# Mixing transform and capacity-limited expert layer on one core: tokens stored by transform call, expert phase in program order, and late tokens packed by top-8

## The chip, the cores and the metric

The kernel runs on one core of one Trainium2 chip. The metric is device time in microseconds (us), and lower is better. Medians are quoted with the range. Before the change the median was 743.34 us (742.24 to 746.65, three runs).

The engines are called as the profile calls them. PE is the matrix engine and PEld its weight loads, which overlap PE. DVE is the vector engine, ACT the scalar engine, POOL the general-purpose engine, and SP the engine that issues plain DMAs. Indirect DMAs, which gather or scatter rows by an index, are all issued from POOL here.

One warning for all numbers below: the runs fell on several chips, and the kernel before took about 742 us on some and about 702 us on others. Every verdict is therefore a ratio to the kernel before on the same chip in the same rounds, and absolute times are compared only within one chip.

## The reference, cut to what matters

```python
def _attn_ref(x):                         # x: 8 x 2496 x 256
    X = np.fft.fft(x, axis=1)
    X = np.fft.fft(X, axis=2)
    return X.real.astype(np.float32)

def _moe_ref(x, w_gate, w1, w2):          # 19968 tokens, 8 experts, 256 -> 1024 -> 256
    cap = N // E                          # 2496 tokens for each expert, exactly
    logits = x @ w_gate
    order = np.argsort(-logits.flatten())
    for idx in order:                     # best (token, expert) pair first
        tok, e = int(idx) // E, int(idx) % E
        if assigned[tok] >= 0 or counts[e] >= cap:
            continue
        assigned[tok] = e
        counts[e] += 1
    ...
    for e in range(E):
        mask = assigned == e
        out[mask] = np.maximum(x[mask] @ w1[e], 0.0) @ w2[e]
```

The input is the same draw each time (`np.random.seed(19597987)`).

## The kernel before

The kernel computes the transform as matmuls with cosine and sine tables and stores the tokens to DRAM (`t_dram`). It finds one threshold per expert in four rounds. A token sits in a grid of 128 partitions by 160 columns. After a part of the first round most tokens are already decided; they are the *early* tokens. Each early token's place is its rank among those of the same expert in the same pair of columns, and 24 places (`SW`) are kept per expert and pair. Whoever doesn't fit, or isn't decided yet, is *late*.

```python
# rank: for output partition k, count the chosen tokens in partitions p > k
nc.vector.tensor_scalar(rankb, in0=kgrid[:, 0:P], scalar1=iota_p, scalar2=None, op0=AL.is_lt)
...
# first_strips(): rank in one column, and for the second column of a pair all of the first on top
nc.tensor.matmul(rps, lhsT=rankb, rhs=ohb[...], start=True, stop=False)
nc.tensor.matmul(rps.rearrange("p (f s k) -> p f s k", s=2, k=NK)[:, :, 1, :], lhsT=onesb,
                 rhs=ohb[...][:, :, 0, :], start=False, stop=True)
...
nc.vector.scalar_tensor_tensor(has, in0=t3, scalar=float(SW), in1=sure, op0=AL.is_lt, op1=AL.mult)  # early
```

The transform's results go to `t_dram` through three stores per batch, and the negated copies have a tile of their own:

```python
st = stg.tile([P, NB, 2, D], BF, tag="stage", bufs=2, name="stage")
sn = stg.tile([P, NB, 2, P], BF, tag="stneg", bufs=2, name="stneg")
...
for b in range(NB):
    dst = td_q[kc, :, b0 + b].rearrange("p (g s) d -> p g s d", s=2)
    nc.sync.dma_start(dst[:, :, 0, :], st[:, b])
    nc.sync.dma_start(dst[:, :, 1, 0:P + 1], st[:, b, :, 0:P + 1])
    nc.sync.dma_start(dst[:, :, 1, P + 1:D], sn[:, b, :, 0:P - 1])
```

A *sort call* reloads 8 columns of tokens (`xl`) and moves them into expert order by matmuls with 0/1 marks (`pt`). The marks of one column are one contiguous row of 192 values:

```python
def sort_call(n):
    ...
    for g in range(4):
        pt = work_tile([P, 2, EW], BF, "pt", 4)
        for cc in range(2):
            nc.vector.tensor_scalar(pt[:, cc, :], in0=rampw, scalar1=spot[:, c:c + 1], scalar2=None,
                                    op0=AL.is_equal)
        for cc in range(2):
            for j2 in range(2):
                nc.tensor.matmul(sps[...], lhsT=xl[:, 2 * g + cc, j2 * P:(j2 + 1) * P],
                                 rhs=pt[:, cc, :], ...)
        take(dst[:, :, 4 * u + g, :], sps[...])
```

`take` evicts a matmul result on ACT or DVE, whichever a running count of work holds less busy. Then come 56 expert tiles of up to 384 tokens: 40 early ones out of the sorted strips, 16 late ones gathered from DRAM. A tile is 16 matmuls with `w1` (`hps`) and 24 with `w2` (`ops`); its result rows (`ot`) go out by three scatters. Between tiles, at fixed places (`aside`), the kernel runs the later rounds, the placing of the late tokens (`rest_step`) and the inverse of that placing (`place_step`), which tells each late slot its token:

```python
at(0, 3, finish_round)
for n in range(NROUND - 1):
    at(2 + 3 * n, 3, round_step)
at(11, 3, rest_step)
at(13, 3, place_step)      # inverse over all 160 columns, then the decode of the indices
G0 = 16                    # first gather of a late tile
```

A flag counts whatever went wrong, such as an expert over its capacity. If it isn't zero, a *fallback* behind `tc.If(unsettled > 0)` decides and computes again all tokens that are not early. It is always right, and slow.

## Time and profile before

| stage of the kernel before (profiled span 747.3 us) | us |
|---|---|
| tables, logits | 0 to 150 |
| transform, from where the weights load too | 150 to 259 |
| weight turns, first sorts | 259 to 286 |
| tiles 0 to 15, with the later rounds | 286 to 405 |
| no `hps` matmul at all (placing, inverse, decode) | 405 to 443 |
| the other 40 tiles | 443 to 747 |

The first lines to read are windows of the trace of the kernel before. The columns are: start and end, length, busy us of each engine with its number of instructions, granted clock of PE (1 is full), DMA share, GB/s.

```profile
core 0: us, PE busy (x) PEld busy (x) DVE busy (x) ACT busy (x) POOL busy (x), PEclk, DMA share, GB/s
202.00:259.00 57.00, 57.00 (x502) 49.33 (x500) 0.00 (x0) 22.37 (x53) 0.00 (x0) 0.97 0.52 121
...
286.00:400.00 114.00, 106.86 (x832) 74.23 (x832) 104.58 (x329) 84.02 (x249) 48.17 (x41) 0.94 0.32 90
400.00:441.00 41.00, 22.35 (x196) 18.95 (x194) 31.94 (x61) 4.56 (x19) 0.37 (x1) 0.60 0.01 4
...
500.00:615.00 115.00, 115.00 (x969) 88.10 (x967) 54.83 (x138) 67.79 (x157) 59.95 (x61) 1.00 0.26 86
615.00:690.00 75.00, 54.85 (x392) 39.45 (x391) 24.15 (x47) 23.71 (x57) 48.54 (x50) 0.89 0.19 59
```

From 286 to 400 DVE is busy 92% of the time: the rounds run there. In 400 to 441 POOL issues one DMA, because its next instruction is a gather that waits for the inverse. From 500 to 615 PE is the limit. From 615 to 690 PE idles a quarter of the time.

The POOL timeline of the kernel before (start, length, instruction, idle time before it and what ended that) shows the gather that waits, and the pace of indirect DMAs after it:

```profile
441.65 1.02 POOL L921 DMA_INDIRECT xg<-t_dram,ids_l  x1 [41.27 <-DVE wa L638]
442.97 0.98 POOL L921 DMA_INDIRECT xg<-t_dram,ids_l  x1 [0.30 <-issue]
444.26 0.95 POOL L921 DMA_INDIRECT xg<-t_dram,ids_l  x1 [0.30 <-issue]
```

Note how to read this: one indirect DMA counts 0.98 us busy, but the next starts 1.3 us after it.

In the chain of waits of the kernel before (start, length, what), the stores of the transform stand between 160 and 202:

```profile
168.07 8.91 DMA t_dram<-stage
...
177.00 9.35 DMA t_dram<-stneg
...
188.28 9.42 DMA t_dram<-stneg
```

The groups of instructions of the sort, kernel before (form, count, busy us, mean ns of one, idle time before and its causes):

```profile
L870 DVE TENSOR_SCALAR pt<-rampw,spot 128x192 bf16<-128x192 bf16 x160 | 39.5, 308 | 66.2 <-PE sps L875 60.7 <-DMA t_dram<-stneg 2.5 <-issue 1.1
L875 PE MATMUL sps<-pt,xl 128*128 128x192 bf16 x320 | 34.5, 255 | 7.6 <-DMA xl<-t_dram 3.5 <-ACT hb L783 2.3 <-DVE w1t L789 1.1
```

The mean of a pipelined matmul (255 ns) includes its latency. What a matmul costs in a stream is its start-to-start time. It follows from a burst on the PE timeline, here 16 sort matmuls without a gap:

```profile
508.98 1.48 PE L875 MATMUL sps<-pt,xl 128*128 128x192 bf16 x16
```

That is (1.48 - 0.255) / 15 = 0.082 us each. The Trainium skill, "TensorE: Matmul & The Clock Gate", section "Back-to-back issue gap", gives N / 2.4 + 2.5 ns for the gap of an isolated matmul at a warm clock, by which I estimate 82.5 ns for N = 192. The section says that in a stream of weight loads and matmuls the formula is off; this burst is such a stream, and yet its trace agrees with the formula.

### The profile page before, as it was taken

What the parts mean: (1) busy time and instruction counts of PE and PEld (TensorE: products, weight loads), DVE (VectorE), ACT (ScalarE), POOL (GpSimd) and SP (SyncE); (2) the same over time, 40 slices, a digit from 0 to 9 for tenths busy, and PEclk for the clock granted to TensorE, in tenths of its full rate; (3) what the DMA queues carried; (4) which work ended last, traced back from release to release, by engine and by line L of the source; (5) the groups of instructions that cost most, each with busy time, mean ns of one, the idle gap of its engine ahead of it and who ended that gap; (6) DMA issues with size and microseconds to landing.
All of it is one profiled execution on the core that took longest, in us unless ns stands there. A gap on an engine that the chain in (4) does not pass through costs nothing.

```text
span 747.3 us, 12493 instructions
## 1 busy us (share of the span) xinstructions
PE 585.3 (78%) x4496; PEld 414.1 (55%) x4496; DVE 396.5 (53%) x958; ACT 373.2 (50%) x878; POOL 330.7 (44%) x364
## 2 busy tenths in 40 slices
PE   0766766668699968998987475489999997767994
PEld 0322321657588835666664453267777775545773
DVE  3986884568000086988997860103564553323552
ACT  1677886442233444767875013277555442323552
POOL 8786722270000040534533027645545557665554
PEclk9999796889999997999999557789999999799998
DMA  8676510069954595422221002222311222111111
GB/s 273 229 217 188 188 31 0 2 111 190 176 118 116 123 225 141 118 76 71 92 74 59 1 21 89 82 83 94 120 69 64 76 73 71 55 54 62 62 56 50
DMA packets 82854, 74.71 MB, mean 100 GB/s; under 512 B 28195, under 2 KB 67149, under 8 KB 82784
## 3 DMA queue, kind: packets, MB, share of 16 engines
q0 software_dynamic: 23296, 42.10, 21.4%
q1 hardware_dynamic: 59488, 31.74, 16.2%
q8 instruction: 37, 0.61, 0.3%
q14 instruction: 33, 0.27, 0.1%
HBM read 51.26 MB, written 32.24 MB: 112 GB/s over the span
## 4 chain that ended last, share of the span: by engine, by line
PE 50%; ACT 13%; DVE 12%; issue 7%; DMA 7%; POOL 6%; another core or an unknown queue 3%; SPq 0%; POOLq 0%; DVEq 0%; ACTq 0%
PE hps L945 15%; PE ops L956 13%; PE fftps L807 8%; PE yps L270 5%; POOL out_dram L960 4%; DMA t_dram<-stneg 3%; PE sps L875 3%; ACT zball L255 2%; ACT cjunk L474 2%; DMA t_dram<-stage 2%; DVE o_lo L602 2%; ACT zt L269 1%; ACT hb L783 1%; PE inv_ps L618 1%
## 5 line engine op out<-in xcount | busy, mean ns | idle before, releaser
L956 PE MATMUL ops<-w2t,hb 128*128 128x256 bf16 (+1 forms) x1344 | 185.9, 281 | 2.8 <-ACT hb L783 1.9
L960 POOL DMA_INDIRECT out_dram<-ot,rid x120 | 127.6, 1064 | 126.2 <-ACT ot L783 72.0
L783 ACT ACTIVATE hb<-hps 128x384 bf16<-128x384 f32 (+1 forms) x303 | 138.1, 490 | 67.2 <-PE hps L945 48.6
L956 PEld LDWEIGHTS <-hb 128*128 128x128 bf16 (+1 forms) x1344 | 135.9, 102 | 41.7 <-issue 4.8
L945 PE MATMUL hps<-xs,w1t 128*128 128x384 bf16 x640 | 136.3, 341 | 19.7 <-ACT hb L783 7.1
L945 PEld LDWEIGHTS <-w1t 128*128 128x128 bf16 x896 | 89.3, 101 | 89.5 <-issue 52.3
L787 DVE TENSOR_SCALAR hb<-hps 128x384 bf16<-128x384 f32 (+1 forms) x145 | 79.0, 548 | 76.7 <-PE hps L945 47.7
L783 ACT ACTIVATE ot<-ops 128x256 f32<-128x256 f32 (+1 forms) x121 | 46.2, 382 | 134.9 <-PE ops L956 83.1
L870 DVE TENSOR_SCALAR pt<-rampw,spot 128x192 bf16<-128x192 bf16 x160 | 39.5, 308 | 66.2 <-PE sps L875 60.7
L270 PE MATMUL yps<-zt,g_sb 128*16 128x512 f32 (+1 forms) x96 | 48.6, 612 | 32.1 <-ACT zt L269 30.9
L921 POOL DMA_INDIRECT xg<-t_dram,ids_l x48 | 46.2, 962 | 56.8 <-DVE wa L638 41.3
L945 PE MATMUL hps<-xt,w1t 128*128 128x384 bf16 (+1 forms) x256 | 53.0, 335 | 20.1 <-issue 8.4
L960 POOL DMA_INDIRECT out_dram<-ot,rows_l x48 | 47.0, 979 | 39.9 <-ACT ot L783 29.4
L111 POOL DMA_INDIRECT xb<-in_x_dram,mir_i x40 | 51.5, 1288 | 20.3 <-issue 15.2
L810 ACT CAST stage<-fftps 128x512 bf16<-128x512 f32 x40 | 23.3, 584 | 68.7 <-PE fftps L807 35.5
L827 POOL DMA_DIRECT2D w1raw<-in_moe_w_dram x8 | 5.9, 734 | 114.7 <-PE wps L836 114.0
L807 PE MATMUL fftps<-zball,hi_cE 128*128 128x258 bf16 (+1 forms) x200 | 48.1, 279 | 8.5 <-ACT stneg L811 7.3
L807 PE MATMUL fftps<-zball,hi_sO 128*128 128x254 bf16 (+1 forms) x200 | 47.0, 275 | 0.0
L789 DVE CAST w1t<-wps 128x512 bf16<-128x512 f32 x11 | 7.5, 685 | 73.9 <-PE misc L515 73.7
L875 PE MATMUL sps<-pt,xl 128*128 128x192 bf16 x320 | 34.5, 255 | 7.6 <-DMA xl<-t_dram 3.5
L783 ACT ACTIVATE xs<-sps 128x384 bf16<-128x384 f32 x69 | 30.6, 492 | 16.5 <-PE sps L875 12.5
L267 PEld LDWEIGHTS tp<-identf,z 128*128 128x128 f32 x160 | 19.6, 157 | 33.7 <-issue 27.8
(296 smaller groups left out, 942.5 us busy)
## 6 DMA issues: line engine op xcount, KB each, us to landing
xl<-t_dram SPq DMA_DIRECT2D x20, 512.0 KB
xa<-in_x_dram SPq DMA_DIRECT2D x8, 1024.0 KB
t_dram<-stage SPq DMA_DIRECT2D x40, 128.0 KB
w1raw<-in_moe_w_dram POOLq DMA_DIRECT2D x8, 512.0 KB
w2t<-in_moe_w_dram POOLq DMA_DIRECT2D x8, 512.0 KB
t_dram<-stage SPq DMA_DIRECT2D x40, 64.5 KB
t_dram<-stneg SPq DMA_DIRECT2D x40, 63.5 KB
out_dram<-ot,rid POOLq DMA_INDIRECT x120
```

Source lines behind the costliest of these rows:

```text
L111: nc.gpsimd.indirect_dma_start(out=bv[0:n, i, :], out_offset=None, in_=x_pairs, in_offset=bass.IndirectOffsetOnAxis(ap=mir_i[0:n, b * NK + ...
L270: nc.tensor.matmul(yps[pb:pb + 2 * E, 0:nn, :], lhsT=g_sb[:, blk, :], rhs=zt[:, 0:nn, :], start=(blk == 0), stop=(blk == 1))
L783: nc.scalar.activation(dst, src, ACT.Relu if relu else ACT.Copy)
L787: nc.vector.tensor_scalar(dst, in0=src, scalar1=0.0, scalar2=None, op0=AL.max)
L807: nc.tensor.matmul(fps[:, :, d0:d1], lhsT=tabs_[r][:nv, i, ks], rhs=zball[:nv, b0:b0 + NB, 2 * i + r, d0:d1], start=(i == 0 and r == 0), s ...
L810: nc.scalar.copy(st[:, :, sg, :], fps)
L870: nc.vector.tensor_scalar(pt[:, cc, :], in0=rampw, scalar1=spot[:, c:c + 1], scalar2=None, op0=AL.is_equal)
L875: nc.tensor.matmul(sps[:, j2 * EW:(j2 + 1) * EW], lhsT=xl[:, 2 * g + cc, j2 * P:(j2 + 1) * P], rhs=pt[:, cc, :], start=(cc == 0 and j2 == ...
L921: nc.gpsimd.indirect_dma_start(out=xg[0:nr, q, :], out_offset=None, in_=t_dram, in_offset=bass.IndirectOffsetOnAxis(ap=d["ids"](q, nr), ax ...
L945: nc.tensor.matmul(hps[:, 0:n], lhsT=w1t[d["e"]][:, j2, fc * P:(fc + 1) * P], rhs=d["x"](j2), start=(j2 == 0), stop=(j2 == 1))
L956: nc.tensor.matmul(ops[0:nr, 0:D], lhsT=d["hid"][:, fc, b0:b0 + nr], rhs=w2t[d["e"]][:, fc, :], start=(fc == 0), stop=(fc == F // P - 1))
L960: put = nc.gpsimd.indirect_dma_start(out=out, out_offset=bass.IndirectOffsetOnAxis(ap=d["rows"](b0 // P)[0:nr], axis=0), in_=ot[0:nr, :], ...
```

## The change

The intent has four parts. (1) The transform writes each half call with one store in 1 KB runs from a ring of five buffers, so that stores hold up nothing. (2) One DVE instruction makes the marks of all 8 columns of a sort call. (3) The expert phase keeps program order on PE, DVE, ACT and POOL (`manual_schedule`; before, the language's own scheduler ordered each engine's instructions); the later rounds are generators cut at `yield`, and `pace()` runs a piece of about 1.4 us of DVE after each third of a tile. (4) The late tokens of each partition are packed by top-8 steps into 64 slots (`KC`), so that the inverse covers 64 columns rather than 160; if a partition has more, the flag is raised.

The diff, cut to its core (the conversion of the rounds to generators, index arithmetic and set-up moved to other places are left out):

```diff
+KC = 64
+SYNC = None
 ...
     def transform(n):
-        st = stg.tile([P, NB, 2, D], BF, tag="stage", bufs=2, name="stage")
-        sn = stg.tile([P, NB, 2, P], BF, tag="stneg", bufs=2, name="stneg")
         for sg in range(2):
+            st = stg.tile([P, NB, 2, D], BF, tag="stage", bufs=5, name="stage")
             ...
-        for b in range(NB):                       # three stores per batch
-            ...
+            nc.scalar.copy(st[:, :, 0, :], fps)
+            nc.scalar.activation(st[:, :, 1, P + 1:D], fps[:, :, P + 1:D], ACT.Copy, bias=0.0, scale=-1.0)
+            nc.gpsimd.tensor_copy(st[:, :, 1, 0:P + 1], st[:, :, 0, 0:P + 1])
+            nc.sync.dma_start(td_v[n].rearrange(...)[:, :, sg, :], st.rearrange("p b s d -> p b (s d)"))
 ...
+    def sort_mark(n):
+        marks[n] = work_tile([P, EW, 8], BF, "pt", 2)
+        nc.vector.tensor_tensor(marks[n], ramp8, spot[:, None, 8 * n:8 * n + 8].to_broadcast([P, EW, 8]),
+                                op=AL.is_equal)
-                                     rhs=pt[:, cc, :], start=(cc == 0 and j2 == 0), ...
+                                     rhs=pt[:, :, 2 * g + cc], start=(cc == 0 and j2 == 0), ...
 ...
     def settle_rest():        # was rest_step() and place_step()
+        nc.vector.tensor_scalar(sure, in0=sl["has"], ..., accum_out=full)     # late tokens of a partition
+        nc.vector.tensor_scalar(full, in0=full, scalar1=KC + 0.5, scalar2=None, op0=AL.is_gt)
+        nc.vector.tensor_tensor(over_n, over_n, full, op=AL.add)
+        set_flag(flag_i, over_n)
+        for r in range(KC // 8):
+            nc.vector.max(keys[:, 8 * r:8 * r + 8], key)
+            if r < KC // 8 - 1:
+                nc.vector.match_replace(out=key, in_to_replace=keys[:, 8 * r:8 * r + 8], in_values=key, ...)
+            yield 0.6
+        yield from inverse(hi_l, lo_l, pay_l, E * LB, KC)       # 8 columns per piece
 ...
-    G0 = 16
+    G0 = 28
+        at(j, 1, lambda d=d: (place_all(), gather(d)))          # runs whatever pieces remain
+    def pace():
+        credit[0] = min(credit[0] + 1.4, 1.4)
+        while credit[0] > 0.0:
+            c = next(todo, "end")
+            ...
+            if c is SYNC:
+                return
+            credit[0] -= c
+    with tc.manual_schedule(engines=MAN):
         ...
         experts(tiles + late, "rows_out", aside, 0, pace)
```

## The prediction

> **What bounds the kernel now** (page and stage windows of the profile; span 747.3 us).
>
> 1. 0–150 us: tables, logits. Almost unchanged.
> 2. 150–259: transform, 800 matmuls. From 202 they run back to back, 0.11 us each: 88 us would do. Between 160 and 202 the chain of waits shows stores of `stage`/`stneg` to DRAM (9 us each; two buffers) while weights load. About 18 us lost.
> 3. 259–286: weight turns; the first sort waits for stores and reloads (`xl`).
> 4. 286–745: 56 expert tiles. At full pace (500–615: PE busy 115 of 115, clock 1.00) a tile costs PE 16 x 0.163 + 24 x 0.107 = 5.2 us. Elsewhere that isn't kept:
>  - 286–400: threshold rounds; DVE busy 92%; about 7.9 us per tile.
>  - 400–441: rest and inverse, DVE and PE alternating; no expert matmul for some 33 us (clock 0.60).
>  - 441–500: four tiles in 59 us. POOL stood 41 us behind the first late gather (waiting for the decode), then issues gathers and scatters back to back, 1.3 us each.
>  - 615–690: POOL again, 6 x 1.3 = 7.8 us per tile; PE busy 55 of 75.
>
> **What the change does**
> - Stores: one per half call, 1 KB runs, five buffers; reloads in 4 KB runs. Price: a POOL copy of 258 elements per half, about 0.4 us (estimate from the 2048-element copy, 1.90), hidden. Transform should become PE-bound: -12 us; stage 3: -8.
> - Sort marks: 8 instructions of 0.31 us become one of about 0.95 (estimate from `o_lo`, 2048 elements in 1.22): -1.5 us of DVE per call.
> - The sort matmuls then read every eighth bf16, 16 B apart. The Trainium skill, "SBUF — State Buffer", note on cachelines, wants two hits per 16-byte line for full rate. The trace shows strided operands only in the inverse, at half clock, no penalty visible. If halved: +0.083 x 320 = 26 us; I count 6.
> - Inverse: 160 columns to 64 (8 pieces, 1.3 us DVE each), plus 8 top-8 steps of 0.6: about 10 us DVE less, and cut up.
> - Rounds paced, 1.4 us of DVE per third of a tile. By the yields I count 101 pieces; the first gather forces the remainder at tile 28 (after 84). A burst of about 15 us remains, where 33 were lost.
> - Late gathers start at tile 28, spaced, after the decode: the 441–500 loss (about 35) mostly goes. But POOL must do 48 gathers and 84 scatters from tile 28 on: 172 us at 1.3, against PE's 150. POOL bounds the end; 615–690 stays.
>
> **Sum.** Experts start at 265. Tiles 0–27: ACT+DVE work about 330 us over two engines, 6.9 us per tile: to 458. Burst 15. Tiles 28–55: 185. End 658.
>
> **Prediction: 658 us, 8 in 10 within 626 to 696; faster by over 2%: 0.94, within 2%: 0.03, slower: 0.03.**
>
> **What would show it.** No `t_dram` stores of 9 us in the chain at 160–202; last transform matmul near 245; first `hps` near 265; no 20 us without expert matmuls; tiles 0–27 at 6.5 to 7.2 us with DVE and ACT both above 80%; POOL above 85% from tile 28 to 48; sort matmuls' start-to-start at 0.083 us (no stride price) or more.
>
> **What would make it wrong.** In-order queues: a paced piece ahead of an eviction stalls PE each third of a tile (up to 696). The stride costing 26 us or more. POOL copies or the 1536-element ramp holding the transform or the first sort. More than 64 late tokens in a partition: the fallback runs, far slower. Or the rounds hide fully and tiles run near 6.0 (about 630).

## The result, and the profile after

The change doubled the time. All four runs of the kernel after, and the profiled run of the kernel before, are on record as fast.

| | median us | range | runs | profiled span, mean granted clock |
|---|---|---|---|---|
| before | 742.79 | 741.49 to 746.65 | 4 | 747.3 us, 0.901 |
| after | 1518.84 | 1515.55 to 1528.28 | 4 | 1518.6 us, 0.821 |

The ratio is 2.045, with a 95% interval of 2.033 to 2.057. A ratio here is the mean time of one kernel's fast runs over that of the other's fast runs of the same rounds, so it is not quite the ratio of the medians. The record of this set does not say whether its result is correct; e13_room72 below, which takes the same slow path, is correct.

The windows of the trace after, columns as before:

```profile
202.00:251.00 49.00, 49.00 (x443) 42.90 (x443) 0.00 (x0) 19.16 (x44) 9.00 (x22) 1.00 0.36 119
251.00:291.00 40.00, 32.55 (x99) 11.41 (x99) 12.48 (x20) 11.55 (x23) 7.03 (x8) 0.59 0.58 145
291.00:541.00 250.00, 243.59 (x1541) 145.81 (x1546) 152.34 (x369) 150.13 (x395) 90.53 (x84) 0.98 0.24 76
541.00:564.00 23.00, 6.87 (x62) 5.96 (x62) 18.51 (x63) 0.00 (x0) 0.88 (x1) 0.58 0.02 6
564.00:780.00 216.00, 179.19 (x1296) 126.17 (x1293) 88.68 (x200) 79.31 (x173) 130.87 (x132) 0.93 0.19 59
780.00:1000.00 220.00, 71.26 (x250) 37.57 (x251) 163.72 (x376) 26.75 (x134) 11.79 (x13) 0.50 0.02 4
1000.00:1518.00 518.00, 363.22 (x2475) 248.02 (x2472) 172.74 (x360) 143.36 (x299) 306.89 (x311) 0.82 0.24 30
```

Two things stand out. The work that should end the kernel is done by 780; 738 us follow, first 220 us of DVE work, then 518 us with POOL running 311 instructions, nearly all of them indirect DMAs. And from 251 to 541 PE is busy 276 of 290 us while a tile takes longer than before: PE is busy with something slow.

The groups of the trace after name both:

```profile
L1043 POOL DMA_INDIRECT out_dram<-ot,rows_c x160 | 159.4, 996 | 132.5 <-ACT ot L858 53.3 <-DVE ot L864 46.8 <-issue 24.1
L1004 POOL DMA_INDIRECT xg<-t_dram,ids_c x160 | 156.2, 977 | 276.7 <-DVE wa L671 204.8 <-issue 42.3 <-PE tp L1016 12.4
...
L952 PE MATMUL sps<-pt,xl 128*128 128x192 bf16 x320 | 114.1, 517 | 0.4 <-ACT ot L858 0.4
...
L938 DVE TENSOR_TENSOR pt<-ramp,spot 128x1536 bf16<-128x1536 bf16 x20 | 19.0, 950 | 0.6 <-POOL ramp L923 0.6
```

`ids_c` and `rows_c` exist only in the fallback: 160 gathers and 160 scatters there mean that the flag was raised. And the 320 sort matmuls, same count and shape as before, are busy 114.1 us in place of 34.5. The marks did become cheaper as intended: 0.95 us per call where 8 x 0.308 = 2.5 us stood.

The PE timeline after shows the sort matmuls at two clocks:

```profile
269.01 21.95 PE L952 MATMUL sps<-pt,xl 128*128 128x192 bf16 x64
...
403.62 2.88 PE L952 MATMUL sps<-pt,xl 128*128 128x192 bf16 x8
```

The burst of 8 gives (2.88 - 0.517) / 7 = 0.338 us start to start, 4.1 times the 0.082 of before; the granted clock there was 1.00 (402 to 408). The burst of 64 gives (21.95 - 0.517) / 63 = 0.340, and there the granted clock was 0.50 with PE shown busy 20.00 of 20 us (270 to 290). The same pace at half and at full clock suggests that the matmuls wait for their operand and not for the array; the experiments on the stride below test it.

### The profile page after: what moved, and what is told of

It is laid out like the page before. It is cut to its first block, busy times and chain, and to the rows that moved or that the text cites. A ratio compares the mean times of both kernels' runs of the same rounds, so it can differ in the third digit from the quotient of the medians.

```text
span 1518.6 us, 19800 instructions
## 1 busy us (share of the span) xinstructions
PE 1080.0 (71%) x7117; PEld 696.8 (46%) x7123; DVE 737.7 (49%) x1633; ACT 544.7 (36%) x1286; POOL 665.8 (44%) x729
## 5 line engine op out<-in xcount | busy, mean ns | idle before, releaser
L1039 PE MATMUL ops<-w2t,hb 128*128 128x256 bf16 (+2 forms) x2624 | 374.7, 289 | 84.2 <-issue 35.5
L862 DVE TENSOR_SCALAR hb<-hps 128x384 bf16<-128x384 f32 (+2 forms) x432 | 224.0, 535 | 332.8 <-PE hps L1028 171.0
L1039 PEld LDWEIGHTS <-hb 128*128 128x128 bf16 (+2 forms) x2624 | 272.4, 104 | 176.4 <-issue 108.5
L1028 PE MATMUL hps<-xt,w1t 128*128 128x384 bf16 (+2 forms) x1152 | 250.0, 349 | 81.9 <-DVE hb L862 40.1
L858 ACT ACTIVATE hb<-hps 128x384 bf16<-128x384 f32 (+2 forms) x464 | 210.3, 480 | 243.4 <-PE hps L1028 161.6
L1028 PEld LDWEIGHTS <-w1t 128*128 128x128 bf16 x1792 | 180.7, 104 | 215.9 <-issue 152.6
L1004 POOL DMA_INDIRECT xg<-t_dram,ids_c x160 | 156.2, 977 | 276.7 <-DVE wa L671 204.8
L1043 POOL DMA_INDIRECT out_dram<-ot,rows_c x160 | 159.4, 996 | 132.5 <-ACT ot L858 53.3
L858 ACT ACTIVATE ot<-ops 128x256 f32<-128x256 f32 (+2 forms) x184 | 70.7, 384 | 195.4 <-PE ops L1039 89.2
L952 PE MATMUL sps<-pt,xl 128*128 128x192 bf16 x320 | 114.1, 517 | 0.4 <-ACT ot L858 0.4
```

The costliest lines, as they stand in the source:

```text
L858: nc.scalar.activation(dst, src, ACT.Relu if relu else ACT.Copy)
L862: nc.vector.tensor_scalar(dst, in0=src, scalar1=0.0, scalar2=None, op0=AL.max)
L952: nc.tensor.matmul(sps[:, j2 * EW:(j2 + 1) * EW], lhsT=xl[:, 2 * g + cc, j2 * P:(j2 + 1) * P], rhs=pt[:, :, 2 * g + cc], start=(cc == 0 an ...
L1004: nc.gpsimd.indirect_dma_start(out=xg[0:nr, q, :], out_offset=None, in_=t_dram, in_offset=bass.IndirectOffsetOnAxis(ap=d["ids"](q, nr), ax ...
L1028: nc.tensor.matmul(hps[:, 0:n], lhsT=w1t[d["e"]][:, j2, fc * P:(fc + 1) * P], rhs=d["x"](j2), start=(j2 == 0), stop=(j2 == 1))
L1039: nc.tensor.matmul(ops[0:nr, 0:D], lhsT=d["hid"][:, fc, b0:b0 + nr], rhs=w2t[d["e"]][:, fc, :], start=(fc == 0), stop=(fc == F // P - 1))
```

## The experiments

Fifteen runs were made, in five groups; each group shares a chip and its runs of the kernel before. "Before here" is that kernel's median on the same chip. All timed runs were correct except one. The theories were these. Theory A: the doubling is the fallback, because the packing has too few slots per partition, and the rest is the stride of 16 bytes with which a sort matmul reads its marks. Rivals: the fallback runs for another reason (a bug in the packing, or an expert over capacity); the slow sorts come from program order, from waiting evictions or from the clock.

### Room for all late tokens: e1_room

```diff
-KC = 64
+KC = 88
-        ki = asg.tile([P, KC], I32, name="ki")
+        ki = wa[:, 3, 0:KC].bitcast(I32)          # scratch moved into rows of wa: SBUF was full
-        kt = [asg.tile([P, KC], I32, name="kt%d" % i) for i in range(3)]
-        some = asg.tile([P, KC], FT, name="some")
+        kt = [wa[:, i, 0:KC].bitcast(I32) for i in range(3)]
+        some = wa[:, 4, 0:KC]
```

> Room for 88 late tokens per partition in place of 64 (scratch tiles put into a free tile, so that it fits); else the changed kernel. Theory 'overflow': placing the reference's tokens by the kernel's rule gives 23 partitions with more than 64 late tokens, at most 79, so the flag is raised by the count alone. Then the fallback is gone, the result stays right and the time is about 788 us: the hot part's end at 778 plus three more inverse pieces of 1.74 us, three more top-8 steps of 0.77 us and the end of the program. Rival 'rounds': the paced rounds leave an expert over capacity, or an expert's list is too long; then the fallback stays and the time is 1525 us or more. In both cases the sort matmuls still start every 0.34 us.

Measured: 760.85 us (758.91 to 762.22), before here 701.64, ratio 1.0835 [1.080, 1.087]. No instruction of the fallback is in the trace. The expectation of 788 was stated for the slower kind of chip, so its absolute number does not apply here (on that kind, e14_room80 below took 801); what it said, no fallback and unchanged sort matmuls, held. Two things changed in this edit, the room and the scratch tiles; e13_room72 and e14_room80 tell them apart. With enough room the packing gives the right result, and the capacity of the experts was not the cause. The sort is unchanged at 114.1 us busy.

### The stride of the sort's marks: e2_s8, e3_s4, e4_s2

All three start from e1_room and change only how the marks lie in memory: a step of 8, 4 or 2 bytes between neighbours that one matmul reads, in place of 16.

```diff
-        marks[n] = work_tile([P, EW, 8], BF, "pt", 2)           # step 16 B
+        marks[n] = work_tile([P, 2, EW, 4], BF, "pt", 2)        # e2_s8: step 8 B
+        marks[n] = work_tile([P, 4, EW, 2], BF, "pt", 2)        # e3_s4: step 4 B
+        marks[n] = work_tile([P, 8, EW], BF, "pt", 2)           # e4_s2: contiguous
...
-                                     rhs=pt[:, :, 2 * g + cc], ...
+                                     rhs=pt[:, (2 * g + cc) // 2, :, (2 * g + cc) % 2], ...   # e3_s4
```

> As e1_room, with the marks of four tokens side by side instead of eight: the moving operand of the sort matmuls steps 8 bytes[...]. Theory 'stride'[...]: start-to-start falls from 0.34 us to between 0.083 and 0.17, the kernel to 705 to 735 us. Rival 'eviction' (the sort matmuls wait for PSUM buffers or for the in-order evictions): 0.34 stays and so does the time of e1_room, about 788.

> As e1_room, step 4 bytes[...]. Theory 'stride': start-to-start 0.083 us, kernel about 705 us (80 us less than e1_room). The VectorE mark has inner runs of two, so it may lose its fast rate: 0.95 us, at most 1.9. Rival 'eviction': about 788.

> As e1_room, marks contiguous for PE (step 2 bytes). Theory 'stride': start-to-start 0.083 us as in the kernel before; the VectorE mark gets an operand repeated along its inner dimension, so about 1.9 us (estimate from bt, 768 elements in 0.95) against 0.95, which is off the critical path in most tiles: about 707 us. Rival 'eviction': about 788.

Measured, all on the chip of e1_room; the start-to-start time is worked out from bursts of 8 (2.88, 1.54, 0.85 and 0.82 us long) in the way shown above. One burst of each of the last three, in the order 8, 4 and 2 bytes:

```profile
320.51 1.54 PE L955 MATMUL sps<-pt,xl 128*128 128x192 bf16 x8
...
300.34 0.85 PE L955 MATMUL sps<-pt,xl 128*128 128x192 bf16 x8
...
288.51 0.82 PE L952 MATMUL sps<-pt,xl 128*128 128x192 bf16 x8
```

| marks' step | sort, busy us | start to start, us | DVE per call, us | median us | ratio to before [95%] |
|---|---|---|---|---|---|
| 16 B (e1_room) | 114.1 | 0.338 | 0.95 | 760.85 | 1.0835 [1.080, 1.087] |
| 8 B (e2_s8) | 60.8 | 0.170 | 0.95 | 713.91 | 1.0175 [1.014, 1.021] |
| 4 B (e3_s4) | 34.7 | 0.085 | 0.95 | 693.21 | 0.9879 [0.984, 0.992] |
| 2 B (e4_s2) | 34.2 | 0.081 | 1.75 | 699.98 | 0.9970 [0.994, 1.000] |

The groups of e3_s4:

```profile
L955 PE MATMUL sps<-pt,xl 128*128 128x192 bf16 x320 | 34.7, 252 | 3.0 <-DVE pt L940 2.6 <-ACT ot L858 0.4
...
L940 DVE TENSOR_TENSOR pt<-rampm,spot 128x1536 bf16<-128x1536 bf16 x20 | 19.0, 949 | 0.0
```

The groups of e4_s2:

```profile
L938 DVE TENSOR_TENSOR pt<-rampw,spot 128x1536 bf16<-128x1536 bf16 x20 | 35.0, 1750 | 0.1
...
L952 PE MATMUL sps<-pt,xl 128*128 128x192 bf16 x320 | 34.2, 254 | 6.1 <-DVE pt L938 4.7 <-ACT cjunk L484 1.2 <-DVE s_cand L527 0.2
```

The price of a matmul follows the step, with program order and everything else unchanged: the stride is the cause, and the rivals for the sorts fall. The times of e3_s4 and e4_s2 came out 7 to 12 us below what was expected (about 705 and 707). From 16 to 4 bytes the busy time falls by 79 us and the whole kernel by 68 us. A step of 4 bytes is the best of the four, because the contiguous layout makes the DVE instruction slower (one operand is then broadcast along the inner axis; 1.75 against 0.95 us), and DVE is needed in this stage.

With both defects mended the kernel is only 1.2% faster than before, not the 11.5% that was predicted. The next question is where that gain went.

### The kernel before against itself, with a trace on the faster chip: b_again

No edit.

> The kernel before, unchanged, for its trace on this chip (its time was 743 us on the chip of the prediction and 702 on that of the first experiments). Ratio 1.00. Theory 'output buffers': the difference between chips lies in the last third, where evictions into the eight ot buffers wait for scatters to land; there the stage 500 to the end should show it, and the stages up to 500 us should agree within 10 us. Rival 'clock or DMA everywhere': all stages are shorter in proportion.

Measured: 702.44 us (700.65 to 705.07), before here 705.55, ratio 0.9974 [0.992, 1.003], span 700.1. So the difference between 742 and 702 us belongs to the chips. Its trace is the one to hold against those of the mended kernel. Counted from the first `hps` matmul, the tiles start at the same times as in the first trace, within 0.1 us, up to tile 15. Then this chip is 31 us ahead at tile 18, just after the first late gathers, 19 at tile 22, and 41 at the end. That is a partial miss: the expectation wanted agreement within 10 us up to 500 us and the whole difference after it. Windows of the trace of b_again:

```profile
400.00:425.00 25.00, 10.96 (x101) 9.85 (x100) 22.36 (x42) 0.00 (x0) 0.00 (x0) 0.59 0.00 1
425.00:500.00 75.00, 62.34 (x485) 47.46 (x485) 21.08 (x73) 41.44 (x105) 49.56 (x51) 0.86 0.32 95
625.00:697.00 72.00, 59.00 (x494) 46.20 (x491) 29.58 (x58) 29.17 (x69) 49.93 (x52) 0.98 0.23 73
```

### More of the rounds per third of a tile: e6_pace

From e3_s4, with the pieces larger, so that none is left when the first gather forces them.

```diff
-    G0 = 28
+    G0 = 26
-        credit[0] = min(credit[0] + 1.4, 1.4)
+        credit[0] = min(credit[0] + 2.4, 2.4)
```

> As e3_s4 (ratio 0.988), with 2.4 us of VectorE work let through per third of a tile in place of 1.4, and the first late gather at tile 26 instead of 28. By the yields the rest is then placed after 75 calls, at tile 25, so nothing is left to force. Theory 'burst' (the remainder forced at tile 28 stops the expert matmuls for the 33 us that e3_s4 shows at 475 to 515): about 20 to 30 us faster than e3_s4, ratio 0.95 to 0.96, no window of 10 us without expert matmuls. Rival 'evictions': longer pieces ahead of the evictions cost about as much per tile as the burst did, ratio 0.98 to 1.0.

Measured: 689.67 us (685.78 to 691.7), before here 705.55, ratio 0.9772 [0.972, 0.983]. The long stretch without expert matmuls is gone (between 400 and 560 no gap between `hps` matmuls exceeds 5.1 us), but tiles 0 to 25 now take about 8.3 us each, where they take 7.0 in e12_again below. Against the ratio of e3_s4 (0.9879, another chip) this is some 1.1%, about a third of the expected gain and nearer to the rival's range: the work of the rounds didn't vanish, it moved into the tiles.

### The scheduler's order in place of program order: e7_sched

From e3_s4.

```diff
-    with tc.manual_schedule(engines=MAN):
+    if True:
```

> As e3_s4, but the expert phase is ordered by the scheduler again instead of in program order (undoes that part alone). Theory 'order matters': the scheduler pulls the rounds, and with them the rest and the inverse, ahead and lets them hold PE, as in the kernel before: 10 to 40 us slower than e3_s4, ratio 1.00 to 1.05. Rival: the pieces carry all of the effect, the order none; within 1% of e3_s4.

Measured: 683.09 us (679.12 to 684.75), before here 705.55, ratio 0.9685 [0.963, 0.974]. That is a miss with the wrong sign: the part of the change that was meant to keep the engines in step costs about 2%. The theory that program order is what makes the pacing work falls.

### Without the packing: e8_nopack

From e3_s4; the inverse again covers all 160 columns, in paced pieces of 8.

```diff
-        for r in range(KC // 8):
-            nc.vector.max(keys[:, 8 * r:8 * r + 8], key)
-            ...
-        yield from inverse(hi_l, lo_l, pay_l, E * LB, KC)
+        hi_l = asg.tile([P, GC], BF, name="l_hi")
+        lo_l = asg.tile([P, GC], BF, name="l_lo")
+        nc.vector.scalar_tensor_tensor(hi_l, in0=sl["v"], scalar=1.0, in1=sl["has"], op0=AL.add, op1=AL.mult)
+        nc.vector.tensor_scalar(lo_l, in0=sl["lo"], scalar1=1.0, scalar2=None, op0=AL.add)
+        yield from inverse(hi_l, lo_l, payb, E * LB, GC)
```

> As e3_s4 without the packing by top-8: the inverse runs over all 160 columns in 20 pieces instead of 11 (undoes that part alone; no count can overflow). Nine more pieces of 1.74 us, less eleven top-8 steps of 0.77 and about 3 us of decoding the packed keys: 4 to 6 us slower, ratio about 0.995, if the packing is worth only what it saves; more than 15 us slower if the length of the forced burst costs doubly (PE clock falling to half while it lasts).

Measured: 699.69 us (697.94 to 702.96), before here 705.55, ratio 0.9936 [0.988, 0.999]. Against the ratio of e3_s4 on two other chips (0.9879, and 0.9895 below) the packing may be worth some 0.5%, about 4 us, as was expected, but the intervals overlap ([0.984, 0.992] and [0.988, 0.999]) and the chips differ, so this is not shown. It is also the part that brought the fallback.

### Placing spread over thirty tiles: e9_late30 and e10_late30s, with e12_again beside them

From e3_s4: the first gather at tile 30 and 1.8 us of DVE per piece, so that the pieces just run out in time. e10_late30s is the same in the scheduler's order. e12_again is e3_s4 without an edit, on this chip.

```diff
-    G0 = 28
+    G0 = 30
-        credit[0] = min(credit[0] + 1.4, 1.4)
+        credit[0] = min(credit[0] + 1.8, 1.8)
-    with tc.manual_schedule(engines=MAN):         # e10_late30s only
+    if True:
```

> As e3_s4 (room for 88, marks 4 bytes apart, program order), with 1.8 us of VectorE work per third of a tile in place of 1.4 and the first late gather at tile 30 instead of 28: by the yields the rest is placed after 88 calls, at tile 29.3, so nothing is left to be forced. Theory 'burst': e3_s4 lost 33 to 40 us at tile 28 to the forced remainder; most of it comes back, 655 to 670 us where e3_s4 takes 693. Rival 'evictions' (as e6_pace hinted): the larger pieces slow every tile before, 685 us or more.

> As e9_late30, ordered by the scheduler instead of in program order. e7_sched was 14 us faster than e3_s4 by the medians, so about 645 to 660 us if the two gains add; equal to e9_late30 if the scheduler's gain was only in the forced burst.

> The kernel of e3_s4 once more, so that the three others are compared with it on one chip: ratio 0.98 to 0.99 of the kernel before on a chip like the last two; about 0.96 on one like that of the prediction, where the kernel before loses some 40 us more in its late stage.

| before here 702.58 | median us | range | ratio to before [95%] |
|---|---|---|---|
| e12_again | 694.51 | 691.16 to 700.34 | 0.9895 [0.981, 0.998] |
| e9_late30 | 678.49 | 677.07 to 685.55 | 0.9645 [0.958, 0.971] |
| e10_late30s | 657.70 | 655.19 to 658.37 | 0.9361 [0.930, 0.942] |

e9_late30 was expected at 655 to 670 if the burst was the cost and at 685 or more if the larger pieces were; it fell between. e10_late30s was expected at 645 to 660 and hit. So larger pieces with a later first gather, which end the burst, were worth about 16 us on balance, and program order costs about 21 us here; e7_sched had shown the sign, with 14.

What the order costs can be read between 285 and 475. Windows and waits of e9_late30 (a wait line names the waiting instruction, the releaser, the total us, the times and the longest):

```profile
285.00:475.00 190.00, 174.63 (x1389) 127.31 (x1393) 149.68 (x392) 139.46 (x383) 78.27 (x75) 0.97 0.29 90
```

```profile
PE misc L491 <- ACT cnt_x L488: 5.3, 3, 2.5
```

The same of e10_late30s:

```profile
285.00:475.00 190.00, 186.97 (x1567) 141.78 (x1569) 149.19 (x398) 144.00 (x404) 89.09 (x83) 1.00 0.30 97
```

```profile
PE misc L491 <- ACT cnt_x L488: 0.9, 2, 0.6
```

In program order PE stands at a small matmul of a round (`misc`) until DVE and ACT have made its operand, with the expert matmuls queued behind it. In the scheduler's order other matmuls stand there. PE is busy 187 rather than 175 of 190 us, and the first 26 tiles take 176 us from the first `hps` matmul rather than 195. The two traces exaggerate a little: that of e9_late30 is the slowest of its five runs (685.55), that of e10_late30s the fastest of its four (655.19), and e10_late30s's transform, which the edit doesn't touch, ended 5 us earlier. The `misc` wait shown is one of several such waits; it alone does not make up the 12 us.

### Fewer gathers: e11_gather1

From e9_late30: each late tile gathers once and uses the rows three times. The result is wrong (relative error 0.44); only the time is of interest.

```diff
-        for q in range((d["n"] + P - 1) // P):
+        for q in range(1):
...
-                nc.tensor.transpose(tp[:, j2, q * P:q * P + nr], xg[0:nr, q, j2 * P:(j2 + 1) * P],
+                nc.tensor.transpose(tp[:, j2, q * P:q * P + nr], xg[0:nr, 0, j2 * P:(j2 + 1) * P],
```

> Wrong result on purpose: as e9_late30, but each late tile gathers only its first 128 rows and uses them three times, so POOL issues 16 gathers instead of 48 and all else stays. Theory 'POOL rate' (from the first late gather on, POOL's 1.28 us for each gather or scatter sets the pace): 32 x 1.28 = 41 us less POOL work, and the end comes 20 to 40 us earlier than in e9_late30, until PE's 5.2 us per tile takes over. Rival 'landing' (the eight output buffers wait for the scatters' own latency): the same time as e9_late30 within 8 us.

Measured: 666.95 us (666.47 to 675.67), before here 702.58, ratio 0.9530 [0.944, 0.962]. That is 12 us less than e9_late30 by the medians and 19 by the profiled spans (683.5 and 664.8; the first is of the slowest run of its set). By the medians it lies between the two theories, which expected 20 to 40 and at most 8. Late stage and waits of e9_late30:

```profile
575.00:650.00 75.00, 61.34 (x460) 45.31 (x459) 29.22 (x60) 26.10 (x60) 57.23 (x59) 0.91 0.24 71
```

```profile
ACT ot L858 <- DMA out_dram<-ot,rows_l: 32.6, 12, 4.9
```

Late stage of e11_gather1, and what is left of the same wait in that window:

```profile
575.00:650.00 75.00, 74.61 (x631) 59.04 (x628) 40.69 (x81) 38.74 (x81) 47.22 (x49) 1.00 0.20 66
```

```profile
ACT ot L858 <- DMA out_dram<-ot,rows_l: 0.7, 1, 0.7
```

This supports a mechanism of the late stage. In e9_late30 POOL runs 59 instructions in 75 us, nearly all of them indirect DMAs, one each 1.27 us, which is its full pace. Scatters queue behind gathers, so the `ot` buffers come free late; ACT waits up to 4.9 us for one, and the evictions behind it in ACT's queue wait too. Take 32 of the 48 gathers away, and PE goes from 61 to 75 busy of 75 us. The edit takes away POOL's issuing and the gathers' traffic at once, so which of the two delays the scatters is not shown.

### Where the threshold of the fallback lies: e13_room72 and e14_room80

e1_room with 72 and 80 slots, one look each (one execution, state unknown).

```diff
-KC = 88
+KC = 72          # e13_room72
+KC = 80          # e14_room80
```

> As e1_room with room for 72 in place of 88: the same edit of the scratch tiles, only the number differs. Theory 'overflow' (placing the reference's tokens by the kernel's rule gives at most 79 in one partition): 72 still overflows, the fallback runs, the result is right and the time is above 1400 us. Rival 'side effect' (the fallback went away in e1_room because of the moved scratch tiles, not of the room): about 760 us.

> As e1_room with room for 80. Theory 'overflow', with my maximum of 79: no fallback, right result, about 758 us. If the kernel's more cautious first choice leaves a partition with more than 80, the fallback runs and the time is above 1400 us; the count in my placement is then too low by one or two, and the theory holds with another maximum.

Measured: 1529.01 us with 72 slots, 801.05 with 80, the kernel before 742.21 on the same chip; both correct. The fallback's gathers and scatters are in the trace of the first and not in that of the second. The 758 us expected for 80 slots was the number of the faster chip. The rival "side effect" falls, for both kernels have the moved scratch tiles. The 728 us between them are the fallback's price. To say in advance where the threshold should lie, I placed the reference's tokens on the host by the kernel's rule. That gives 4761 late tokens, 37 per partition on average, but 23 partitions with more than 64 and a largest count of 79. (A second count on the host gave 4697, 37, 23 and 78; the kernel's own counts stand in no trace.) The threshold between 72 and 80 agrees with both.

### The best version on the slower kind of chip: e15_best

The kernel of e10_late30s, unchanged.

> The kernel of e10_late30s once more, on whatever chip comes. On a chip where the kernel before takes about 702 us: ratio 0.93 to 0.94, as then. On one where it takes about 742: its last stage is longer by some 30 us there too, as in e14_room80 (801 where e1_room took 761), so about 690 to 700 us, ratio 0.93 to 0.95.

Measured: 701.4 us (699.64 to 712.14; one of the four runs was slow), before here 742.81, ratio 0.9452 [0.936, 0.954] from the fast runs, as expected (0.93 to 0.95, about 690 to 700 us). So the change with the marks at a step of 4 bytes, 88 slots, the first gather at tile 30, 1.8 us per piece and the scheduler's order is 5 to 6% faster than the kernel before on both kinds of chip.

## Why the prediction was wrong

The prediction was 658 us with a range of 626 to 696; the result was 1518.84. The terms in order of size:

1. **The fallback, +728 us (shown: e1_room, e13_room72, e14_room80).** The step that failed is "More than 64 late tokens in a partition: the fallback runs, far slower." The prediction wrote this down as a risk and left it out of its 658. All slower outcomes together were given a chance of 0.03. The profile before doesn't show the count, but it needed no run. As an estimate from the layout: in a pair of columns about 32 of 256 tokens want each expert, for 24 places; the second column ranks behind the whole first one, and a low partition behind the higher ones. A token of partition 0 in a second column thus has around 31 ahead of it. There are 80 second columns, so the first partitions can have up to about 80 late tokens each, and the measured threshold between 72 and 80 fits. The average of 37 hides it. A limit that holds per partition has to be checked against the worst partition.

2. **The stride, +79 us of PE time, +68 us of the whole (shown: e1_room against e3_s4).** The prediction said: "If halved: +0.083 x 320 = 26 us; I count 6." The trace shows 0.338 us per matmul, not 0.166, so 0.256 x 320 = 82 us by start-to-start times, and most of it lay on the critical path, because PE was the limit in that stage. The mechanism was named and its term mis-sized. The prediction took from the Trainium skill, "SBUF — State Buffer", the note on cachelines, that the full rate needs two hits per 16-byte line. Here one hit per line costs 4.1 times, two hits still 2.1 times, and only four per line (4 bytes) come within 5% of the contiguous rate. Halving was the prediction's own assumption; the page only says that there is a penalty. And the inverse, in which the prediction saw none, could not have shown it: its matmuls have 48 columns and came one each 0.10 us (32 in 3.23 us in b_again), while the price found here, 0.338 / 192 = 1.76 ns per column, is 0.085 us for 48.

3. **What remains with both mended: 692.2 us (span of e12_again) where 658 was predicted.** The 658 was worked out from a trace of the slower kind of chip, and no run timed both mends there with this order and pace. An estimate from e14_room80's 801.05 less the 68 of the stride is 733 us, so about 75 us are missing there, not 34. The stages of e12_again are in these windows:

```profile
283.00:473.00 190.00, 178.85 (x1457) 132.35 (x1461) 144.24 (x346) 139.61 (x380) 86.69 (x81) 0.99 0.30 96
473.00:515.00 42.00, 20.07 (x153) 15.75 (x151) 33.89 (x122) 6.34 (x15) 7.02 (x7) 0.59 0.05 17
515.00:600.00 85.00, 85.00 (x713) 65.08 (x712) 47.20 (x96) 43.27 (x95) 63.64 (x65) 1.00 0.25 79
600.00:650.00 50.00, 39.12 (x294) 28.32 (x291) 17.97 (x38) 15.77 (x36) 38.08 (x39) 0.93 0.23 68
650.00:690.00 40.00, 31.35 (x263) 24.80 (x261) 16.32 (x33) 16.67 (x36) 26.06 (x27) 0.93 0.23 75
```

| stage, e12_again | predicted us | measured us |
|---|---|---|
| until the first `hps` matmul | 265 | 280 |
| tiles 0 to 27 | 193 (6.9 each) | 190 for 27 tiles (7.0 each); 197 until the burst |
| burst at the first gather | 15 | 33 without `hps` (476.4 to 509.2); 42 for the window, with 1.3 tiles in it |
| from the end of the burst to the end of the span | 185 | 183 (509.2 to 692.2) |

- *"Transform should become PE-bound: -12 us; stage 3: -8"* failed by about 15 us. The last transform matmul ended at 250.9 in the trace after where it ended at 258.9 in that of the kernel before, and on the faster kind of chip at 251.0 (e12_again) where b_again has 253.1, with a scatter from 247.8 to 254.0 among the runs with the new stores. So 2 to 8 us came of the 12, and before's 8.9 to 9.4 us stores were worth less than they seemed in the chain: the weights still load in that stage, and the DMA share from 150 to 202 is still 1.01 (1.07 before). From there to the first `hps` it takes 29 us where b_again takes 27: the weight turns wait twice for `w1raw`, 3.7 and 3.2 us. These causes were read from the traces, not tested. The chain of waits found in the trace after doesn't reach back to the transform, so it can't answer the first item of "what would show it".
- *"A burst of about 15 us remains, where 33 were lost"* failed as to size. The stretch without `hps` matmuls is 37 us in the kernel before on either kind of chip (398.9 to 436.4 in b_again), 33 us in e12_again with 88 slots, and 25 us in the trace after with the 64 slots that were predicted (539.3 to 564.3). The hole moved from tile 15 to tile 28 and shrank by 5 to 12 us, not by the 18 that were predicted. The pieces left over are those that alternate between DVE and PE (one piece of the inverse follows the other every 1.74 us), and once forced they run one after another with no expert work between. e9_late30 removes the burst and gains 16 us.
- *Tiles 0 to 27 at 6.9 us* was right within the reading. But DVE and ACT were 76% and 73% busy there, not both above 80%: PE, busy 179 of 190 us, was nearer to the limit than the sum of ACT and DVE work had it.
- *"POOL bounds the end; 615-690 stays"* was right in kind, as e11_gather1 supports. Its size, 185 us, fits the faster chip (183 in e12_again), but on the slower kind, from whose trace it was read, the same stretch takes 216 us in the trace after and 225 in e14_room80 (574.1 to 799.0): 31 to 40 us more. The sign asked for (POOL above 85% busy) was a poor one, because POOL at full pace shows as 77%: 38.08 of 50 us (76%) from 600 to 650.
- *"The 441–500 loss (about 35) mostly goes"* held at its place only: on the slower kind of chip e14_room80 stays within 4 us of e1_room up to tile 34, so the jump after the first late gathers is gone, but it falls behind by 38 us until the end.
- *"In-order queues: a paced piece ahead of an eviction stalls PE"* was right as a danger. It costs about 14 to 21 us (e7_sched against the ratio of e3_s4, e10_late30s against e9_late30), which no line of the predicted sum held.

What stays open: why the same kernel takes 742 us on some chips and 702 on others. e15_best and e10_late30s are one kernel on both kinds, and their tiles start at the same times from the first `hps` matmul, within 0.1 us, up to tile 28; after the first late gathers (477 us, tile 29) the slower chip loses 32 us by tile 32 and 44 us by the end. As in the two traces of the kernel before, the difference begins only after the first late gathers, wherever they stand. The traces of the slower kind lack many records of where POOL's DMAs landed (waits that stand as `DMA out_dram` in e10_late30s stand as `remote` in e15_best), so they can't tell what the engines wait for. The cause stays open.

## What to carry to other kernels

When a change adds a limit per partition with a slow path behind it, work out the worst partition by the kernel's own placing rule on the real input before you think about microseconds: an average of 37 against 64 slots said nothing. When one instruction is merged on one engine, look at how the other engine then reads the result; a layout with pairs of bf16 adjacent kept the cheap DVE instruction and, within 5%, the full matmul rate. And put waiting work of other engines into a tile only if something may pass it: cut fine enough to end before it is needed, and in an order in which the matmuls behind it need not stand.

## What the Trainium skill lacked or had wrong

- "SBUF — State Buffer", note on cachelines under "Door 1: The DMA port swizzle" (its first statement also in "Advanced Engine Details and Errata", "SBUF Cachelines"): full bandwidth is said to need two hits per 16-byte line, and striding to be free up to 8 bf16. For PE's moving operand, 128 partitions by 192 bf16, the runs show 0.081 us per matmul contiguous, 0.085 at a step of 2 bf16, 0.170 at 4 (two hits per line) and 0.338 at 8. So nearly free ends at 2 bf16, two hits per line are not enough, and from 2 to 8 bf16 the time doubles with the step.
- "TensorE: Matmul & The Clock Gate", "Back-to-back issue gap": the formula has no term for the stride of the moving operand. The estimate of 82.5 ns for 192 columns, which the section calls a gap of isolated matmuls, the contiguous stream meets (0.081 to 0.082 us) and the step of 8 bf16 misses by 4.1 times. The pace was the same at a granted clock of 0.50 (0.340) and of 1.00 (0.338).
- The same page, Part 1 on the clock gate, says that busy-ness of PE releases the full clock. In the trace after, PE is shown busy 20.00 of 20 us (270 to 290) with slow strided matmuls, and the granted clock stays at 0.50; it was 0.50 for 19 to 22 of the 22 us of the same 64 matmuls in e1_room, e13_room72 and e14_room80 too (in e13_room72 it fell from 1.00 three us after they began), and 1.00 for all 9 us of them in e3_s4. Busy in the profile's sense is not the activity that the gate sees; which it is, no run here tells.
- "GPSIMD Engine Reference" and "DMA: Bandwidth & Descriptors": I found no figure for how fast POOL can issue indirect DMAs of 128 rows. The traces show one each 1.27 to 1.3 us, of which 0.98 is counted as busy, and that pace bounds the last third of this kernel.
- I found no page that mentions chips to differ this much: the kernel before had medians of 701.64 to 705.55 us on three (11, 3 and 4), and 742 to 743 us on chip 2 and in the sets of the prediction.
